# A feature-attention plus Fourier-mixing kernel: the first batch's k, q and v by the hardware queue and TensorE, the trigonometric tables in one chain each, and a new order

## The chip, the cores and the metric

The kernel runs on one core of a Trainium2 chip. The metric is the device time of one execution in microseconds (us), the median of several runs. PE is TensorE, PEld its weight loads, DVE VectorE, ACT ScalarE, POOL GpSimd, SP SyncE.

## What is computed

For 8 batches, 8 heads, 576 positions and 64 columns a head, an attention with a feature map is followed by a Fourier mixing and a two-layer network. The reference, cut to what matters:

```python
def phi(x):
    proj = np.einsum('bhsd,df->bhsf', x, w_phi)          # 64 -> 128
    proj = proj - np.max(np.abs(proj), axis=-1, keepdims=True)
    return np.concatenate([np.exp(proj), np.exp(-proj)], axis=-1)
q_p, k_p = (phi(q), phi(k))
kv = np.einsum('bhsf,bhsd->bhfd', k_p, v)
z = np.sum(k_p, axis=2)
num = np.einsum('bhsf,bhfd->bhsd', q_p, kv)
den = np.einsum('bhsf,bhf->bhs', q_p, z)[..., None] + 1e-06
x = (num / den)                                          # as (8, 576, 512)
X = np.fft.fft(np.fft.fft(x, axis=1), axis=2)
u = x + np.real(X)
un = (u - mean(u)) / np.sqrt(var(u) + 1e-06)
out = u + np.maximum(un @ w_ch1, 0.0) @ w_ch2            # 512 -> 2048 -> 512
```

## The kernel before

All work is done batch by batch, and two to three batches are under way at once. Each batch is cut into streams of small steps, one letter each (`STREAMS`, line 800): K, V and Q load a batch's k, v and q; B and A turn k and q; T makes the feature products (`keys4`, `keys`, `queries`), R the maxima over keys (`kmax`), S the scaled v (`scale_v4`, `scale_v`), P the maxima over queries (`maxima`); M is the mixing (`heads`, then the two transforms), D the folding of rows, N the normalisation, F the two-layer network (`forward`); C makes the constants and W loads the network's weights. The letters of `START`, `FIRST` and seven times `PERIOD` (lines 21 to 23) are the order in which the steps are written, and each engine works through its own instructions in that order. `NEEDS` says which steps must stand ahead of one, and `TILES` and `BUFS` stand for the PSUM buffers (2 of `pj`, 1 of `pk`, 3 of `pb`): `weave` (line 887) holds a letter back until they allow it.

- Loads. POOL's software queue casts fp32 to bf16 on the way (`load`, line 214). For the first batch (`load_first`, line 256) it writes k, v and q in ten pieces. SP then turns k and q by transposing DMAs (`turn_k`, line 270, into `KT4` and `KT`; `turn_q`, line 281).
- Feature products. `keys` (line 349) multiplies a pair of heads of `KT` with `w_phi` into the PSUM tile `psk`; ACT writes both exponentials (`KPp`, `KPn`, line 361); DVE takes the largest absolute value (`MK`, line 375). ACT then makes the scales from `MK` (line 325), and POOL multiplies v by them into `VCn` and `VCp` (line 330; for the first batch DVE does `VCp`). `keyvalue` (line 536) makes `kv` of one head, and ACT copies it as `kvh` (line 552). Queries go the same way through `psq` (maxima `MQ`, line 419) and `psh` (exponentials `QPHP`, `QPHN`, line 469).
- `combine` (line 555) makes one head's output: products on PE, then `tg`, `cb` and `rd` on DVE (lines 566, 571, 573), then the product into `X` on POOL (line 574). Eight of these are followed by the folds `FEO` (line 507) and `CEO`, `SE` (lines 516, 520), which halve the transforms.
- The transforms are matrix products with the tables `CS`, `SS` (576 positions) and `CD`, `SD` (512 columns): `psD` (line 621), `px`, `pu` (line 643). DVE adds `pu` to `X` (lines 648 to 658).
- `normalise` (line 663): per 128 rows DVE takes the statistics (lines 671, 672) and subtracts the mean into `UN` (line 673), and SP transposes `UN` into `UT`. `forward` (line 706) multiplies `UT` with the first weights into `psf` (line 713), ACT applies the ReLU (line 718), the second product is `pso` (line 725), DVE adds it to `X` (line 731), and SP stores.
- The constants (`constants`, line 123) are made on DVE in five chains of three instructions (lines 169, 173, 177), one for each 128 rows of a table, and ACT takes the absolute value (line 181) and the sines (line 195).

Of the kernel before, what the change touches and what calls it, by code (L numbers as in the profile page):

```python
# [20 lines left out]
START = "TSTRCSTSTCSTTCRMMCTKTCRRMPTMRPSTMTNTMMWVRMMMTTMPCTPWDMBNTTTMRPMMMPQMCTAMMNDTMSNSTTTMMRTTSNQRNMRSTTS"  # L21
FIRST = "PMKPTMTFFMFFPMTPPMFRMTPTMTPTFPFFVTRFMMPPTMFFFMFFFMFFAFFMFFPPFMFFTBMFFFMTFFSNFFFFDFFDFQTFTMTFFFFSFSMTFFFMTMFRFTFNFRTMFTFTFFFFTFRMFTFSFTTTFFSFNTTAFNFFFFNFNM"
PERIOD = "MKFMFMPFFMFPMFFMPVFPMBFMMFMFFMFFFRRMFMFFFMFPFFMFTFMFFTFFFPSFTDFFDFFSNSTTFFMFFFFTNFFFMFTMQMFFTFTRRFMTFFTTFFTFNAFSRFMFSFTTFFTFTFTNFFFFFFFNNM"
# [8 lines left out]
def kernel(  # L32
# [71 lines left out]
    gi = xpool.tile([128, 5, C + 1], I32, tag="X", name="gi")  # L104
    gt = [xpool.tile([128, 5, C + 1], F32, tag="X", name=f"gt{i}") for i in range(2)]
    rc_i = gi[:, 0, 0:C]
    pc_i = const.tile([128, 2], I32, name="pc_i")
    rs_i = const.tile([128, 2, 8, 16], I32, name="rs_i")
    tn_i = const.tile([128, 2, 128], I32, name="tn_i")

    def count():
        nc.gpsimd.iota(pc_i[:, 0:1], pattern=[[1, 1]], base=0, channel_multiplier=1)
        nc.gpsimd.iota(rc_i, pattern=[[1, C]], base=0, channel_multiplier=0)
        for j in range(2):
            nc.gpsimd.iota(
                rs_i[:, j], pattern=[[-32, 8], [2, 16]], base=225 + j, channel_multiplier=0
            )
        for t in range(2):
            nc.gpsimd.iota(
                tn_i[:, t, :], pattern=[[1, 128]], base=0, channel_multiplier=2 * t - 1  # L120
            )

    def constants(b):
        rc = gi[:, 1, 0:C].bitcast(F32)
        rs = gi[:, 2, 0:NK].bitcast(F32)
        pc = const.tile([128, 5], F32, name="pc")
        pn = const.tile([128, 5], F32, name="pn")
        blk = const.tile([128, 3], F32, name="blk")
# [17 lines left out]
        nc.vector.tensor_copy(out=rc, in_=rc_i)
        nc.vector.tensor_scalar_add(out=pc[:, 1:2], in0=pc[:, 0:1], scalar1=1.0)
        nc.vector.tensor_scalar_add(out=pc[:, 2:3], in0=pc[:, 3:4], scalar1=256.0)
        nc.vector.tensor_scalar_add(out=pc[:, 4:5], in0=pc[:, 3:4], scalar1=128.0)
        nc.vector.memset(pc[0:1, 2:3], 0.0)  # L150
        nc.vector.tensor_scalar_mul(out=pn[:, 0:3], in0=pc[:, 0:3], scalar1=1.0 / S)
        nc.vector.tensor_scalar_mul(out=pn[:, 3:5], in0=pc[:, 3:5], scalar1=1.0 / C)
        nc.vector.tensor_copy(out=rs[:, 0:256], in_=rs_i[:].rearrange("p j a r -> p (j a r)"))
        nc.vector.tensor_copy(out=rs[:, 256:NK], in_=rc[:, 256:NK])
        nc.vector.memset(rs[:, 256:257], 0.0)
        sins = []
        for j in (3, 4, 0, 1, 2):
            if j < 3:
                n, w, row, P = S, NK, rs, (128, 128, 64)[j]
                dsin, dcos, sgn = SS[0:P, j, :], CS[0:P, j, :], 1.0  # L160
                place = gt[1], 0, 2 * NK * j
            else:
                n, w, row, P = C, C, rc, 128
                dsin, dcos, sgn = SD[:, j - 3, :], CD[:, j - 3, :], -1.0
                place = gt[0], 0, 2 * C * (j - 3)
            t0, t1 = (gi[0:P, i, 0:w].bitcast(F32) for i in (3, 4))
            at = place[0][0:P].rearrange("p a b -> p (a b)")[:, place[2]:place[2] + 2 * w]
            t2, t3 = at[:, 0:w], at[:, w:2 * w]
            nc.vector.tensor_scalar(
                out=t0, in0=row[0:P, 0:w], scalar1=pn[0:P, j:j + 1], scalar2=MAGIC,  # L170
                op0=ALU.mult, op1=ALU.add,
            )
            nc.vector.tensor_scalar(
                out=t1, in0=t0, scalar1=MAGIC, scalar2=-float(n),
                op0=ALU.subtract, op1=ALU.mult,
            )
            nc.vector.scalar_tensor_tensor(
                out=t2, in0=row[0:P, 0:w], scalar=pc[0:P, j:j + 1], in1=t1,
                op0=ALU.mult, op1=ALU.add,
            )  # L180
            nc.scalar.activation(out=t3, in_=t2, func=AT.Abs)
            sc = 2.0 * np.pi / n * (1.0 - 1e-7)
            sins.append((dsin, t2, sgn * sc, 0.0))
            sins.append((dcos, t3, -sc, halfpi[0:P, :]))
            yield
# [69 lines left out]

    def load_first():
        staged["k", 0], pk_ = make_k(0)
        values[0], pv_ = make_v(0, 2)
        staged[0], pq_ = make_q(0)
        load(pk_, (0, 1, 2))  # L260
        nc.gpsimd.memset(V4P[:], 0.0)
        nc.gpsimd.memset(V4N[:], 0.0)
        load(pv_, (2, 0, 1))
        load(pq_, (0,))
        load(pv_, (3,))
        load(pq_, (1, 2, 3))
# [28 lines left out]
    def features(b):  # L295
# [26 lines left out]
        def scale_v(pr):  # L322
            hs = slice(2 * pr, 2 * pr + 2)
            for sgn, VC in ((1.0, VCn), (-1.0, VCp)):
# [4 lines left out]
                eng = nc.vector if b == 0 and sgn < 0 else nc.gpsimd  # L329
                eng.tensor_tensor(  # L330
# [165 lines left out]
    def heads(b):  # L496
# [18 lines left out]
        def fold_rows(cs):  # L515
# [4 lines left out]
            nc.vector.tensor_tensor(  # L520
# [60 lines left out]
        ready = {7: (0,), 6: (1,), 5: (2,), 3: (3,)} if b else {5: (3,), 6: (2,), 7: (1, 0)}  # L581
# [14 lines left out]
    def mixing(b):  # L596
# [6 lines left out]
        nc.scalar.copy(out=CEO[64:128, 2, :, :], in_=pm[64:128])  # L603
# [12 lines left out]
        ET = fpool.tile([128, 2, NK], BF16, tag="ET", name="ET")  # L616
        for i, mat, dst in ((1, SS, ET), (0, CS, DT)):
# [315 lines left out]
```

## Time and profile before

| | us |
|---|---|
| median of 3 runs | 487.97 |
| lowest and highest of them | 486.59 and 494.0 |
| the profiled execution's own time | 493.06 |
| span of its profile, first to last instruction | 491.2 |
| PE busy in the span | 410.0 (83%) |
| DVE, ACT, POOL busy | 330.3, 301.3, 267.2 |

The profiled execution is one run of its own, longer than the median. The span is what the profiler saw from the first to the last instruction; the rest of the time lies around it. Busy time counts what an engine executes; a busy PE is not PE at its peak. Times in the rows further on are counted from the span's start.

### The profile page before, as it was taken

To read this page: it belongs to the slowest core of one execution; us is meant where nothing else is said; L and a number is where in the kernel's file an instruction comes from. 1 tells how busy PE (TensorE), PEld (TensorE's weight loads), DVE (VectorE), ACT (ScalarE), POOL (GpSimd) and SP (SyncE) were. 2 spreads that over 40 slices of the span, in tenths; PEclk is the share of its full clock that TensorE was granted. 3 is DMA by queue.
4 is the path that set the end of the run, shared out by engine and by line. 5 is a ranking of instruction groups with operands and counts; after the bars stand their busy time and mean duration, and the time that the engine had idled before them with its cause. 6 is when DMAs were issued, how large, how long until landed. Compare 5 with 4: busy or idle time off the path is not lost.

```text
span 491.2 us, 10032 instructions
## 1 busy us (share of the span) xinstructions
PE 410.0 (83%) x3897; PEld 250.1 (51%) x3920; DVE 330.3 (67%) x620; ACT 301.3 (61%) x650; POOL 267.2 (54%) x345
## 2 busy tenths in 40 slices
PE   0257271879999899899998999989998999999995
PEld 0135131657447653575456644764375546844752
DVE  1897759457598778586787759775976676739112
ACT  1559453765885689359764786568844977640820
POOL 9434745834945795559547673679356832730100
PEclk9999996798999999899999999999998999999999
DMA  9979993990549917990879265985499024004304
GB/s 105 140 98 173 203 113 54 98 140 2 48 91 125 126 18 103 131 132 9 93 112 144 39 56 101 152 83 45 82 139 123 2 42 104 1 1 79 67 0 97
DMA packets 116303, 42.68 MB, mean 87 GB/s; under 512 B 92576, under 2 KB 111136, under 8 KB 116256
## 3 DMA queue, kind: packets, MB, share of 16 engines
q0 software_dynamic: 52144, 18.37, 37.1%
q1 hardware_dynamic: 64112, 23.67, 30.8%
q8 instruction: 31, 0.51, 0.5%
q14 instruction: 16, 0.13, 0.1%
HBM read 36.77 MB, written 9.44 MB: 94 GB/s over the span
## 4 chain that ended last, share of the span: by engine, by line
PE 50%; DVE 19%; DMA 16%; ACT 9%; POOL 3%; issue 2%; DVEq 0%; SPq 0%; POOLq 0%; ACTq 0%
PE pso L725 18%; PE psf L713 16%; DMA UT<-UN 8%; DMA QT<-QS 4%; PE psD L621 3%; DVE MK L375 3%; DVE UN L673 3%; ACT HT L718 2%; DMA out_dram<-X 2%; DVE st L671 2%; PE pso L740 2%; PE kv L544 2%; DVE cb L571 2%; POOL X L574 1%; ACT KPp L361 1%
## 5 line engine op out<-in xcount | busy, mean ns | idle before, releaser
L713 PE MATMUL psf<-UT,W1b 128*128 128x288 bf16 x1024 | 153.6, 295 | 8.7 <-DMA UT<-UN 7.4
L718 ACT ACTIVATE HT<-psf 128x288 bf16<-128x288 f32 x256 | 103.3, 413 | 81.8 <-PE psf L713 74.4
L725 PE MATMUL pso<-W2b,HT 128*128 128x512 bf16 x491 | 119.4, 380 | 2.9 <-issue 1.1
L713 PEld LDWEIGHTS <-W1b 128*128 128x128 bf16 x1024 | 94.4, 101 | 35.6 <-DMA UT<-UN 6.2
L574 POOL TENSOR_TENSOR X<-cb,rd 128x320 f32<-128x320 f32 x64 | 45.9, 722 | 62.1 <-DVE rd L573 61.6
L725 PEld LDWEIGHTS <-HT 128*128 128x128 bf16 x512 | 46.2, 98 | 59.7 <-issue 10.7
L330 POOL TENSOR_TENSOR VCn<-VS,VCn 128x512 bf16<-128x512 bf16 x32 | 34.5, 1079 | 51.3 <-ACT VCn L325 49.2
L731 DVE SCALAR_TENSOR_TENSOR X<-pso,rs,X 128x512 f32<-128x512 f32 x32 | 23.9, 746 | 45.7 <-PE pso L725 45.7
L507 POOL TENSOR_TENSOR FEO<-X 128x320 f32<-128x320 f32 x60 | 51.9, 885 | 2.4
L419 DVE TENSOR_REDUCE MQ<-psq 128x8 f32<-128x1024 f32 (+1 forms) x40 | 38.8, 1007 | 19.5 <-PE psq L411 19.4
L375 DVE TENSOR_REDUCE MK<-psk 128x8 f32<-128x1024 f32 x32 | 38.4, 1216 | 5.4 <-ACT KPp L361 5.3
L687 POOL TENSOR_SCALAR VE<-MV 128x5 f32<-128x5 f32 x8 | 3.9, 490 | 59.7 <-DVE MV L672 59.6
L361 ACT ACTIVATE KPp<-psk 128x1024 bf16<-128x1024 f32 x32 | 32.5, 1016 | 6.3 <-PE psk L355 5.7
L469 ACT ACTIVATE QPHP<-psh 128x1024 bf16<-128x1024 f32 x32 | 33.2, 1037 | 4.9 <-PE psh L460 4.9
L361 ACT ACTIVATE KPn<-psk 128x1024 bf16<-128x1024 f32 x32 | 32.4, 1012 | 2.3 <-DVE MK L375 2.3
L469 ACT ACTIVATE QPHN<-psh 128x1024 bf16<-128x1024 f32 x32 | 33.5, 1047 | 0.0
L355 PE MATMUL psk<-wphi,KT 64*128 64x128 bf16 x256 | 14.0, 237 | 19.6 <-DVE MK L375 14.9
L330 POOL TENSOR_TENSOR VCp<-VS,VCp 128x512 bf16<-128x512 bf16 x28 | 30.3, 1084 | 0.0
L559 PEld LDWEIGHTS <-QPHP 128*128 128x128 bf16 x320 | 26.3, 105 | 5.8 <-DVE cb L571 3.8
L552 ACT CAST kvh<-kv 128x130 bf16<-128x130 f32 x64 | 17.1, 272 | 18.6 <-PE kv L548 18.4
L671 DVE BATCH_NORM_STATS2 st<-X 128x6 f32<-128x512 f32 (+1 forms) x40 | 27.4, 684 | 0.3
L216 POOL DMA_DIRECT2D QS<-in_q_dram x32 | 26.4, 836 | 0.3 <-issue 0.3
(387 smaller groups left out, 748.3 us busy)
## 6 DMA issues: line engine op xcount, KB each, us to landing
KS<-in_k_dram POOLq DMA_DIRECT2D x16, 256.0 KB, 7.4
QS<-in_q_dram POOLq DMA_DIRECT2D x16, 256.0 KB, 5.0
out_dram<-X SPq DMA_DIRECT2D x64, 64.0 KB
out_dram<-X SPq DMA_DIRECT2D x16, 256.0 KB
VS<-in_v_dram POOLq DMA_DIRECT2D x7, 512.0 KB, 12.2
W1b<-in_moe_w_ch_dram POOLq DMA_DIRECT2D x1, 2048.0 KB, 12.8
W2b<-in_moe_w_ch_dram POOLq DMA_DIRECT2D x1, 2048.0 KB, 24.1
out_dram<-X SPq DMA_DIRECT2D x8, 126.0 KB
```

The source lines that it names most:

```text
L216: nc.gpsimd.dma_start(out=pieces[i][0], in_=pieces[i][1])
L330: eng.tensor_tensor(out=VC[:, hs, :, 0:D], in0=values[b][0][:, hs, :].rearrange("p h (j d) -> p h j d", d=D), in1=VC[:, hs, :, D:D + 1].to ...
L361: nc.scalar.activation(out=KP[:, hs, :, :].rearrange("p e (jp jj) f -> p jj (e jp) f", jj=2), in_=psk[:], func=AT.Exp, scale=sgn,)
L375: nc.vector.tensor_reduce(out=MK[:, 2 * pr:2 * pr + 2, :].rearrange("p e (jp jj) -> p jj (e jp)", jj=2), in_=tiles[pr][:], axis=AX.X, op=A ...
L419: nc.vector.tensor_reduce(out=o, in_=i[:], axis=AX.X, op=ALU.max, apply_absolute_value=True)
L469: nc.scalar.activation(out=o, in_=psh[:], func=AT.Exp, scale=sgn)
L507: eng.tensor_tensor(out=FEO[:, :, i, a:a + D], in0=X[:, :, a:a + D], in1=X[:, :, C - a:C - a - D:-1], op=op,)
L574: nc.gpsimd.tensor_tensor(out=X[:, :, D * h:D * h + D], in0=cb[:, :, 0:D], in1=rd[:].to_broadcast([128, 5, D]), op=ALU.mult,)
L671: nc.vector.bn_stats(out=st[0:M, :], in_=X[0:M, c, 0:C])
L713: nc.tensor.matmul(ps[:], lhsT=W1b[:, cc, 128 * hh:128 * hh + 128], rhs=UT[:, cc, 288 * hf:288 * hf + 288], start=(cc == 0), stop=(cc == N ...
L718: nc.scalar.activation(out=HT[:, hh, 288 * hf:288 * hf + 288], in_=ps[:], func=AT.Relu)
L725: nc.tensor.matmul(po[:], lhsT=HT[:, hh, 128 * c:128 * c + 128], rhs=W2b[:, hh, :], start=(hh == 0), stop=(hh == NHH - 1),)
```

## The change

The first batch's k, q and v come by SP's hardware queue as fp32, without a cast, into memory that is not yet in use (the second weights' tile `W2b` and the network's tile `HT`). TensorE turns k and q there: ten parts of four 128-column blocks (`turn_part`), each part copied out of PSUM as bf16 by ACT (the first two) or DVE. The steps of these parts are two new streams, G (k) and J (q). v is read as fp32 by the products on POOL, which now makes both `VCn` and `VCp`.

Each kind of table has one chain: the 576-position tables as one tile 960 wide, the 512-column tables for the first 128 rows alone; the second 128 rows are made on POOL from the first by a quarter turn (`CD` and `SD` exchanged, with signs). The last table rows are used to partition 65 instead of 128.

In the first batch, the mean is subtracted by ACT instead of DVE, one fold goes from POOL to DVE, half of `SE` goes from DVE to POOL, and the query weights are made in two halves. P has an empty seventh step for the other batches. The three strings of the order are new.

```diff
-START = "TSTRCSTSTCSTTCRMMCTKTCRRMPTMRPSTMTNTMMWVRMMMTTMPCTPWDMBNTTTMRPMMMPQMCTAMMNDTMSNSTTTMMRTTSNQRNMRSTTS"
+START = "CGGTCRTGGRJJGSSTTTWCSTTTPRMTTTRMTKPJRRSTPRJDMTMJSPQPTMMMTMPMWTMSMTMTMMMTBTMMPVMTRCCMTNNRADTNMTNNSSMSSNMTQTMR"
...
+        t0 = gc[:, C:2 * C]
...
+        nc.vector.tensor_tensor(
+            out=at.rearrange("p (j n) -> p j n", n=NK),
+            in0=rs.unsqueeze(1).to_broadcast([128, 3, NK]),
+            in1=pc[:, 0:3].unsqueeze(2).to_broadcast([128, 3, NK]), op=ALU.mult,
+        )
...
+            nc.gpsimd.tensor_tensor(
+                out=dst[:, 1, a::2].rearrange("p (n t) -> p n t", t=2),
+                in0=src[:, 0, a::2].rearrange("p (n t) -> p n t", t=2),
+                in1=sign, op=ALU.mult,
+            )
...
     def load_first():
-        load(pk_, (0, 1, 2))
...
-        load(pv_, (2, 0, 1))
-        load(pq_, (0,))
-        load(pv_, (3,))
-        load(pq_, (1, 2, 3))
...
+        def put(out, in_):
+            nc.sync.dma_start(out=out, in_=in_)
+
+        put(KF4, k[0, :, 512:576, :].rearrange("h p d -> p h d"))
+        for e in range(2):
+            put(wphi_f[64 * e:64 * e + 64, :], w_phi[:, :])
+        for g in range(2):
+            hs = slice(4 * g, 4 * g + 4)
+            put(KF[:, hs, :], k[0, hs, 0:512, :].rearrange("h (p j) d -> p h (j d)", j=4))
+        for QF, at in ((Q01, 1), (Q23, 320)):
+            put(QF, q[0, :, at:at + 256, :].rearrange("h (p j) d -> p h (j d)", j=2))
...
+    def turn_part(dst, blocks, by_act):
+        P = blocks[0].shape[0]
+        ps = pb.tile([128, 4, P], F32, tag="pb", name="pst")
+        for x, block in enumerate(blocks):
+            nc.tensor.transpose(ps[:, x, :], block, ident[0:P, 0:P])
+        if by_act:
+            nc.scalar.copy(out=dst, in_=ps[:])
+        else:
+            nc.vector.tensor_copy(out=dst, in_=ps[:])
...
-                eng = nc.vector if b == 0 and sgn < 0 else nc.gpsimd
-                eng.tensor_tensor(
+                nc.gpsimd.tensor_tensor(
                     out=VC[:, hs, :, 0:D],
...
-        ready = {7: (0,), 6: (1,), 5: (2,), 3: (3,)} if b else {5: (3,), 6: (2,), 7: (1, 0)}
+        ready = {7: (0,), 6: (1,), 5: (2,), 3: (3,)} if b else {6: (3,), 7: (2, 1, 0)}
...
+            if b == 0:
+                nm = small.tile([128, 1], F32, tag="nm", name="nm")
+                nc.vector.tensor_scalar_mul(out=nm[0:M, :], in0=mv[0:M, c, 0:1], scalar1=-1.0)
+                nc.scalar.activation(
+                    out=UN[0:M, c, :], in_=X[0:M, c, 0:C], func=AT.Identity, bias=nm[0:M, :]
+                )
```

Three places on DVE show the new order. The first is DVE's queue around the first batch's key maxima (`MK` of the pairs of heads). Before, chains of the tables stand between them (`gi`, `gt`):

```order
L169 TENSOR_SCALAR gi<-gi,pn 128x320
L173 TENSOR_SCALAR gi<-gi 128x320
L177 SCALAR_TENSOR_TENSOR gt_119<-gi,pc 128x320
L375 TENSOR_REDUCE MK<-psk 128x2x4
L330 TENSOR_TENSOR VCp<-VS,VCp 128x8x64
L169 TENSOR_SCALAR gi<-gi,pn 128x320
L173 TENSOR_SCALAR gi<-gi 128x320
L177 SCALAR_TENSOR_TENSOR gt_119<-gi,pc 128x320
L169 TENSOR_SCALAR gi<-gi,pn 64x320
```

In the changed kernel the last table instruction and the copies of the transposed parts (`pst`) stand there:

```order
L180 TENSOR_TENSOR gs<-gs 128x960
L456 TENSOR_REDUCE MK_151<-ps_196 128x4
L331 CAST KT<-pst 128x512 x2
L461 TENSOR_REDUCE MK<-psk 128x2x4
L331 CAST QT_143<-pst 128x512
L331 CAST QT_144<-pst 128x512
L331 CAST KT<-pst 128x512
```

All table chains now lie ahead of the first key maximum, `VCp` has left DVE, and five copies of parts came in.

The second is DVE's queue where the first batch's mixed rows (`pu`) arrive and are normalised. Before:

```order
L375 TENSOR_REDUCE MK<-psk 128x2x4
L648 TENSOR_TENSOR X<-pu,X 128x512
L651 TENSOR_TENSOR X<-pu,X 128x511
L654 TENSOR_TENSOR X<-pu,X 128x1
L671 BN_STATS st<-X 128x6
L672 BN_AGGR MV_113<-st 128x2
L673 TENSOR_SCALAR UN<-X,MV_113 128x512
L671 BN_STATS st<-X 128x6
```

Now:

```order
L461 TENSOR_REDUCE MK<-psk 128x2x4
L742 TENSOR_TENSOR X<-pu,X 128x512
L745 TENSOR_TENSOR X<-pu,X 128x511
L748 TENSOR_TENSOR X<-pu,X 128x1
L765 BN_STATS st<-X 128x6
L766 BN_AGGR MV_110<-st 128x2
L769 TENSOR_SCALAR nm<-MV_110 128x1
L765 BN_STATS st<-X 128x6
```

The 512-wide subtraction into `UN` became a one-column negation `nm`, and the subtraction itself stands on ACT.

The third is DVE's queue in a later period, where one batch's second product (`pso`) meets the next batch's statistics. Before:

```order
L673 TENSOR_SCALAR UN<-X,MV_113 128x512
L731 SCALAR_TENSOR_TENSOR X<-pso,rs,X 128x512
L671 BN_STATS st<-X 128x6
L672 BN_AGGR MV_113<-st 128x2
L673 TENSOR_SCALAR UN<-X,MV_113 128x512
L731 SCALAR_TENSOR_TENSOR X<-pso,rs,X 128x512
L747 SCALAR_TENSOR_TENSOR X<-pso,rs,X 64x512 x2
```

Now:

```order
L774 TENSOR_SCALAR UN<-X,MV_110 128x512
L832 SCALAR_TENSOR_TENSOR X<-pso,rs,X 128x512 x2
L765 BN_STATS st<-X 128x6
L766 BN_AGGR MV_110<-st 128x2
L774 TENSOR_SCALAR UN<-X,MV_110 128x512
L848 SCALAR_TENSOR_TENSOR X<-pso,rs,X 64x512 x2
```

The statistics of the fourth 128 rows now stand behind both additions of `pso` instead of between them.

## Rows read from the trace of the kernel before

**Rows 1.** Windows of the whole span: busy us per engine, granted clock, DMA share, GB/s.
```profile
0.00:52.00 52.00, 20.01 (x245) 14.65 (x245) 34.53 (x80) 31.29 (x60) 29.70 (x47) 1.00 1.01 133
52.00:104.00 52.00, 27.47 (x270) 16.58 (x272) 31.37 (x63) 27.22 (x57) 30.06 (x37) 0.87 0.92 114
...
104.00:456.00 352.00, 332.87 (x3194) 200.80 (x3213) 259.32 (x472) 230.57 (x505) 205.72 (x260) 0.98 0.65 80
```

**Rows 2.** Waits between 0 and 100 us, the longest: total, times, longest.
```profile
PE psk L355 <- DVE MK L375: 14.9, 3, 7.1
```

**Rows 3.** Windows of the first batch by stage, columns as in rows 1.
```profile
16.00:44.96 28.96, 14.51 (x172) 10.36 (x169) 23.37 (x35) 21.90 (x46) 13.94 (x16) 1.00 0.85 125
44.96:59.43 14.47, 5.50 (x78) 4.30 (x76) 11.14 (x29) 8.45 (x14) 9.62 (x13) 1.00 1.26 203
59.43:71.25 11.82, 7.29 (x36) 3.00 (x37) 6.59 (x17) 5.11 (x13) 5.50 (x8) 1.00 1.16 152
71.25:87.26 16.01, 5.58 (x63) 3.28 (x62) 15.62 (x29) 7.72 (x15) 9.79 (x12) 0.70 0.42 56
```

**Rows 4.** Timeline from 0 to 45 us: start, us, engine, line, operation, idle time before it.
```profile
0.73 1.23 SPq L80 DMA_DIRECT2D wphi_f<-in_w_phi_dram  x2
...
3.58 0.45 DVE L81 CAST wphi<-wphi_f 128x128 bf16<-128x128 f32 x1 [2.42 <-DMA wphi_f<-in_w_phi_dram]
...
10.66 0.60 ACT L346 ACTIVATE K4p<-ps 128x512 bf16<-128x512 f32 x1 [8.65 <-PE ps L341]
...
16.00 1.02 ACT L361 ACTIVATE KPp<-psk 128x1024 bf16<-128x1024 f32 x1 [4.26 <-PE psk L355]
...
22.38 1.60 POOL L330 TENSOR_TENSOR VCn<-VS,VCn 128x512 bf16<-128x512 bf16 x1 [2.03 <-issue]
...
22.98 1.18 DVE L169 TENSOR_SCALAR gi<-gi,pn 128x320 f32<-128x320 f32 x1
...
42.77 1.03 PE L426 MATMUL pt<-MQ,TURN 128*128 128x16 f32 x4
...
44.96 0.50 DVE L566 TENSOR_TENSOR tg<-pn__521,E 128x325 f32<-128x325 f32 x1 [0.85 <-ACT E L433]
```

**Rows 5.** Windows of two microseconds, for the DMA columns at their right end.
```profile
4.00:6.00 2.00, 0.00 (x0) 0.00 (x0) 0.03 (x1) 0.00 (x0) 2.00 (x4) 1.00 0.98 87
...
44.00:46.00 2.00, 1.07 (x17) 0.79 (x14) 1.11 (x3) 1.98 (x4) 0.00 (x0) 1.00 1.06 217
```

**Rows 6.** Groups by line and form from 0 to 80 us: busy us, mean ns.
```profile
L375 DVE TENSOR_REDUCE MK<-psk 128x8 f32<-128x1024 f32 x6 | 7.3, 1213 | 3.8 <-ACT KPp L361 3.8
L361 ACT ACTIVATE KPp<-psk 128x1024 bf16<-128x1024 f32 x7 | 7.2, 1023 | 4.6 <-PE psk L355 4.6
...
L419 DVE TENSOR_REDUCE MQ<-psq 128x4 f32<-128x512 f32 x8 | 5.1, 681 | 2.2 <-PE psq L411 2.2
...
L330 DVE TENSOR_TENSOR VCp<-VS,VCp 128x512 bf16<-128x512 bf16 x4 | 4.6, 1158 | 2.2 <-ACT VCp L325 2.2
...
L673 DVE TENSOR_SCALAR UN<-X,MV 128x512 bf16<-128x512 f32 x4 | 2.0, 509 | 0.1
...
L181 ACT ACTIVATE gt<-gt 128x512 f32<-128x512 f32 x2 | 1.3, 628 | 0.0
```

**Rows 7.** Timeline from 50 to 88 us: what stands at the bounds of rows 3.
```profile
50.87 0.46 DVE L566 TENSOR_TENSOR tg<-pn__612,E 128x325 f32<-128x325 f32 x1
...
59.43 1.04 DVE L516 TENSOR_TENSOR CEO<-FEO 128x256 bf16<-128x256 f32 x1
...
71.25 0.69 DVE L648 TENSOR_TENSOR X<-pu,X 128x512 f32<-128x512 f32 x1 [0.56 <-PE pu L643]
...
87.26 2.11 PE L713 MATMUL psf<-UT,W1b 128*128 128x288 bf16 x8
```

**Rows 8.** Waits of PE from 152 to 414 us, the longest: total, times, longest.
```profile
PE psf L713 <- DMA UT<-UN: 7.4, 4, 2.3
```

**Rows 9.** Timeline of the last batch's end: an addition of `pso` and the idle time before it.
```profile
480.46 0.75 DVE L731 SCALAR_TENSOR_TENSOR X<-pso,rs,X 128x512 f32<-128x512 f32 x1 [2.70 <-PE pso L725]
```

More of the change, by code (lines that the diff above doesn't have):

```diff
@@ L103 @@
     V4N = const.tile([128, 4, 2, D + 1], BF16, name="V4N")
[L104 to L113 removed]
+    gc, gs, ga = (
+        xpool.tile([128, 5, C + 1], F32, tag="X", name=n)[:].rearrange("p a b -> p (a b)")
+        for n in ("gc", "gs", "ga")
+    )
@@ L114, in count, with count_all @@
+    def count_all():
+        for t in range(2):
+            count(tn[:, t, :], [[1, 128]], 0, 2 * t - 1)
+        nc.vector.tensor_single_scalar(
+            out=ident[:], in_=tn[:, 0, :], scalar=0.0, op=ALU.is_equal
+        )
+        count(pc_i[:, 0:1], [[1, 1]], 0, 1)
+        count(pc[:, 3:4], [[1, 1]], 0, 1)
+        count(rc, [[1, C]], 0, 0)
+        count(pc[:, 0:2], [[1, 2]], 225, 2)
         for j in range(2):
-            nc.gpsimd.iota(
-                rs_i[:, j], pattern=[[-32, 8], [2, 16]], base=225 + j, channel_multiplier=0
-            )
@@ L118, in count @@
[L118 to L121, printed above, removed]
-    def constants(b):
[L124 to L128, printed above, removed]
+            count(
+                rs[:, 128 * j:128 * j + 128].rearrange("p (a r) -> p a r", r=16),
+                [[-32, 8], [2, 16]], 225 + j, 0,
+            )
@@ L154, in constants @@
[L154 to L185, printed above, removed]
@@ new lines, in turn_part, with turn_first_k @@
+    def turn_part(dst, blocks, by_act):
[7 more added lines that the diff above has]
+            nc.vector.tensor_copy(out=dst, in_=ps[:])
+    def turn_first_k(b):
+        KF, KF4 = raw[0][0:2]
+        KT, KT4 = turned_k[0]
+        turn_part(KT4[:], [KF4[:, 2 * x:2 * x + 2, :].rearrange("p h d -> p (h d)") for x in range(4)], True)
+        yield
+        for pr in range(4):
+            turn_part(
+                KT[:, 4 * pr:4 * pr + 4, :],
+                [KF[:, 2 * pr + x // 2, 128 * (x % 2):128 * (x % 2) + 128] for x in range(4)],
+                pr < 1,
+            )
+            yield
@@ L270, in turn_k, with turn_first_q @@
+    def turn_first_q(b):
+        Q01, Q23, QF4 = raw[0][2:5]
+        QT01, QT23, QT4 = turned_q[0]
+        for g in range(2):
+            for QF, QT in ((Q01, QT01), (Q23, QT23)):
+                turn_part(QT[:, 4 * g:4 * g + 4, :], [QF[:, 4 * g + x, :] for x in range(4)], False)
+                yield
+            if g == 0:
+                turn_part(QT4[:], [QF4[:, 2 * x:2 * x + 2, :].rearrange("p h d -> p (h d)") for x in range(4)], False)
+                yield
     def turn_k(KS, KS4):
@@ L519, in fold_rows @@
             )
-            nc.vector.tensor_tensor(
+            eng = nc.gpsimd if b == 0 and cs.start == 0 else nc.vector
+            eng.tensor_tensor(
                 out=SE[:, :, cs], in0=FEO[:, 0:2, 0, cs], in1=FEO[:, 2:4, 0, cs], op=ALU.add
@@ L602, in mixing @@
         )
-        nc.scalar.copy(out=CEO[64:128, 2, :, :], in_=pm[64:128])
+        nc.scalar.copy(out=CEO[64:65, 2, :, :], in_=pm[64:65])
         nc.vector.scalar_tensor_tensor(
@@ L820 @@
         "P": lambda b, i, n: (
-            n("A", b) >= 1 and n("M", b - 2) >= 16 and (i < 5 or n("C", 0) >= 6)
+            n("A", b) >= 1 and n("M", b - 2) >= 16 and (i not in (3, 6) or n("C", 0) >= 3)
+            and (b or n("J", 0) >= (1, 2, 3, 3, 4, 5, 5)[i])
         ),
```

212 lines of the change are left out of this document (145 added, 67 removed).

## The prediction

> **What bounds the kernel now.** I read the windows of the whole span first. From 104 to 456 us PE is busy 332.87 of 352.00 us, so that stretch has little to give; from 0 to 104 it is busy 47.5 of 104 [rows 1]. The changed code lies almost all in that head. Next I read the waits of the head: the longest is PE at a key product `psk`, 14.9 us in three waits for DVE's key maxima `MK` [rows 2]. So DVE's queue sets the pace there, and the stage windows say how closely: from the first key exponential (16.00) to the first combination `tg` (44.96) DVE is busy 23.37 of 28.96 us and ACT 21.90; from the arrival of the mixed rows (71.25) to the first product of the network (87.26) DVE is busy 15.62 of 16.01 [rows 3, 4, 7]. The timeline tells what comes before: ACT sits idle 8.65 us until `K4p` at 10.66, and the first key product's exponential starts at 16.00 [rows 4].
>
> **The sum's frame.** The profiled execution took 493.06 us (span 491.2), the median of the runs is 487.97, 5.1 less. The sum is made against 493.06 and 5.1 is taken off at the end, as the execution-to-execution part.
>
> **Term A, up to the first `tg` (before: 44.96).** SP spends 1.23 us on two loads, 0.62 each, and `w_phi`, issued at 0.73, is used at 3.58, 2.85 us later [rows 4]. The small piece of k is now first, so it is there at about 3.6. The first half of k is the fourth load, issued at 0.73 + 3 x 0.62 = 2.6; with what is ahead of it 0.7 MB have to move. No fp32 copy from memory stands in the trace. The software queue wrote 217 GB/s at its best and 87 while starting [rows 5]: 3.3 or 8.3 us, so landing at 6 or 11. I take 6, since the 87 belong to a queue that was only filling. All 3.6 MB take 17 us at 217, and the last v is there at about 20; the second half of v is wanted later than that.
>
> A part is four transpositions of fp32 blocks. The nearest row is `pt`, two fp32 products in four passes of 0.26 us (1.03 in all) [rows 4]. From below, 288 columns with their weights take 0.26 us (2.11 for eight), 128 at that rate 0.12 [rows 7]; from above two passes, 0.52. A part costs 0.5 to 2.1 us; I take 1.2, a little over one pass a block. So k's first full part is ready at 7.2, its copy on ACT (0.63, as a 512-wide pass over SBUF [rows 6]) at 7.8, then `K4p`, `K4n` 0.60 each and the 960-wide absolute value (0.63 x 960 / 512 = 1.2): the first `KPp` starts at 10.2 instead of 16.00.
>
> From there to `tg` it took 28.96 us, 5.6 more than DVE's 23.37. What is each engine's work now? DVE loses `VCp` (4.6) and eleven table instructions that lay in this stretch (at 0.6 each, half of the one in rows 4, 7), and gains eight copies of parts (at most 0.63 each, 5.0): about 17. ACT loses up to five absolute values (3.1) and two 1.02 us exponentials that now stand behind `tg`: about 17. POOL takes over the four `VCp` at 1.16: 13.94 + 4.6 = 18.6, with the next batch's q loads for its v loads [rows 3, 6]. The busiest is now POOL with 18.6. I keep the 5.6 us of waits, because a new one replaces the old: twenty transpositions (five parts, letters GGRJJG, 6 us) stand on PE between the first and the second key product, while ACT has about 4 us of other work. So `tg` comes at 10.2 + 18.6 + 5.6 = 34.4. A = 10.6. Bounds: parts at 2.1 put 0.9 + 4.5 us back (5.2); parts at 0.5 and half of the waits gone give 14.
>
> The Trainium skill ("TensorE: Matmul & The Clock Gate", Part 4: PE-mode transpose) gives about 275 ns for a 128x128 transposition in a kernel (390 alone), of bf16; that would be 1.1 a part, and A would be 11.2. No row here shows one.
>
> One row speaks against the move of work beside POOL: a 320-wide pass on DVE took 1.18 us beside a `VCn` on POOL that itself took 1.60 [rows 4], where the 512-wide subtraction into `UN` on DVE takes 0.51 [rows 6]. The Trainium skill ("SBUF — State Buffer", Who interferes with whom) has DVE and GpSimd share one pair of ports, so that one fully blocks the other. The row agrees. By that rule the 960-wide chain, which now runs beside POOL's counting and clearing, would be some 1.5 us longer, and A 9.1.
>
> **Term B, from `tg` to the mixed rows (26.29 us).** A combination takes (50.87 - 44.96) / 5 = 1.18 us [rows 4, 7], eight of them 9.5, and they still do. The other 5.0 us of the first window [rows 3] are the folds, each of which waited for `X` on POOL between the last combinations. Now all but one stand behind the eighth; `X` (0.7) and five half-microsecond folds on DVE make 3.4. That is 1.6 gained. In the second window the clearing of table rows and half of `SE` leave DVE (some 1.9), but two `MK` of 1.21 come in: 0.5 lost. The quarter turns on POOL are hidden behind these; if they were not, they would be late by their four products of about half a `VCp`, 2.3 us. B = 1.1, bounds -1.5 and 3.
>
> **Term C, from there to the network (16.01 us).** DVE is the bound. Five subtractions of 0.51 go to ACT, five one-column negations (0.1) come: 2.0. Two of the three `MK` of this window now lie ahead: 2.4 [rows 6]. C = 4.4. ACT takes 5 x 0.63 = 3.1 us more in a window where it is busy 7.72 of 16.01 [rows 3]: covered. Without cover it is back to 1.3; and if the network starts as soon as its first three transposed row blocks are there, ahead of the last statistics, 6.5.
>
> **Given back.** Of the ten query maxima of the second batch some four (0.6 each) ran ahead of the network's start on DVE; now all stand behind: 2.4. What follows is bound by PE at 95% [rows 1], so the rest of the gain reaches the end. The new order of the periods I cost at nothing: the wait for `UT`, 7.4 us in four waits [rows 8], can go or be doubled.
>
> **Sum.** 10.6 + 1.1 + 4.4 - 2.4 = 13.7; 493.06 - 13.7 = 479.4, less 5.1 is 474. A change under 2%, 9.8 us, is about what a measurement of this kernel cannot tell from none; 478.2 is that line.
>
> **Rivals.**
> 1. The first loads or the transpositions become the wait. For it: no fp32 load is in the trace, its runs are 256 to 1024 bytes, and five parts stand between two key products. At 87 GB/s q would land at 30 and the last v at 44, `tg` would follow at about 47, and A = -2: total 493.06 - (-2 + 1.1 + 4.4 - 2.4) - 5.1 = 487. Parts at 2.1 us give A = 5.2 and 480. Against: 217 GB/s were written while the source gave twice that in fp32. Between the two, 484.
> 2. Slower: the period's order. In each later batch DVE now takes the statistics of the fourth 128 rows behind both additions of `pso` instead of between them. If those rows' `UT` is what the second half of the network waits for, each batch waits one block of `pso` longer, 2.70 + 0.75 = 3.45 us [rows 9]. For seven batches that is 24 us: 474 + 24 = 498. It outweighs the gain of the head from 2 us a batch. Against: the last 64 rows of `UT` come later still and have kept their place, and the wait for `UT` was under 2 us a batch.
> 3. More than forecast: A 14, B 1.1 and C 6.5, with the waits for `UT` halved (3.7): 493.06 - 5.1 - 22.9 = 465.
>
> **Chances.** Forecast 0.60 (468 to 479), rival 1 0.22 (479 to 488), rival 2 0.05, rival 3 0.13. Faster by over 2% takes the forecast but for its edge, rival 3 and the best end of rival 1: 0.70; within 2% the rest of rival 1: 0.25; slower 0.05. The range 465 to 485 leaves out rival 2, the worst of rival 1 and a little below.
>
> **What would show it.** In the profile after: `K4p` starts near 8 and the first `KPp` near 10; twenty transpositions take 4 to 8 us; `tg` starts at 32 to 37; the first `psf` 14 to 18 us earlier than 87.26; PE's share from there to the end as before; and the distance from the first `psf` to the end at most 3 us longer than 404. It is wrong if `tg` is later than 40 (rival 1: then PE or a load is named before `psk`), or if the head is shorter and the distance from `psf` to the end longer by as much (rival 2: PE's wait for `UT` above 20 us).

## The result, and the profile after

| | before | after |
|---|---|---|
| median (lowest to highest), us | 488.42 (486.59 to 494.0) | 461.56 (458.98 to 463.53) |
| ratio, 95% interval | | 0.9459 [0.9382, 0.9536] |
| profiled execution, its span | 493.06, 491.2 | 458.98, 457.1 |

The change gains 26.9 us between the medians; the forecast was 14, its range ended at 465. Between the two profiled executions the difference is 34.1. (The ratios compare fast executions alone; left out are, among others, one of e1 with 1372 us, one of e18 with 492.5 and two of the five of e12 with 600 at a granted clock of 0.65 throughout, of which e12's profile is one and is not read.)

The windows of the changed kernel that answer to [rows 1]:

```profile
0.00:52.00 52.00, 29.79 (x325) 21.72 (x325) 40.44 (x82) 36.77 (x67) 36.92 (x65) 0.71 1.09 177
52.00:104.00 52.00, 40.09 (x439) 25.82 (x442) 34.91 (x69) 35.40 (x80) 34.64 (x49) 0.83 0.80 100
104.00:456.00 352.00, 339.48 (x3178) 202.31 (x3197) 246.91 (x448) 230.99 (x505) 195.81 (x245) 1.00 0.60 82
```

PE does 22.4 us more of its work ahead of 104. But it is also busier behind 104, at a granted clock of 1.00 instead of 0.98, where I had said that PE's share stays. The stages of the changed kernel, bounded by the same events as in [rows 3] (first `KPp`, first `tg`, first `CEO`, first `X`, first `psf`, end):

```profile
10.49:33.48 22.99, 17.33 (x196) 12.77 (x194) 16.66 (x26) 18.31 (x40) 17.17 (x20) 0.70 0.91 182
33.48:47.51 14.03, 7.04 (x98) 5.61 (x99) 12.16 (x31) 11.44 (x16) 10.78 (x15) 0.59 1.61 145
47.51:60.12 12.61, 7.30 (x28) 2.49 (x29) 6.51 (x11) 5.64 (x12) 8.84 (x19) 0.51 1.30 190
60.12:69.04 8.92, 3.10 (x34) 1.48 (x33) 7.96 (x22) 5.80 (x13) 7.25 (x8) 0.87 0.28 54
69.04:457.10 388.06, 370.46 (x3558) 224.29 (x3580) 271.84 (x490) 257.17 (x567) 218.67 (x276) 0.99 0.61 83
```

The column of the granted clock cannot be compared between the two kernels here: before, it reads 1.00 up to 71 us, yet eight 128-column products take 0.61 us there (`psk` at 21.05), as long as in the changed kernel under 0.50 (`psq` at 20.82).

The last stretch in the kernel before:

```profile
87.26:491.20 403.94, 375.79 (x3542) 228.13 (x3561) 268.74 (x486) 255.77 (x562) 216.37 (x273) 0.98 0.63 78
```

Stage by stage, beside the terms of the sum:

| | before | after | gain | forecast |
|---|---|---|---|---|
| A, start to first `tg` | 44.96 | 33.48 | 11.5 | 10.6 |
| B, to the first `X` | 26.29 | 26.64 | -0.35 | 1.1 |
| C, to the first `psf` | 16.01 | 8.92 | 7.1 | 4.4 |
| from there to the end | 403.94 | 388.06 | 15.9 | -2.4 |
| sum | | | 34.1 | 13.7 |

So the head was read nearly right, and the miss lies behind the first `psf`, where 10.5 us of the 15.9 are PE's idle time (28.15 to 17.60) and 5.3 its busy time. The longest waits of PE between 104 and 456 us, in the kernel before:

```profile
PE psf L713 <- DMA UT<-UN: 7.4, 4, 2.3
PE psq L411 <- DMA QT<-QS: 3.5, 4, 1.8
PE ph L439 <- DVE MK L375: 2.3, 4, 0.6
```

and in the changed kernel:

```profile
PE ps L427 <- DMA KT<-KS: 1.4, 1, 1.4
PE psq L497 <- DMA QT<-QS: 1.4, 2, 0.7
PE psf L814 <- DMA UT<-UN: 1.1, 2, 0.9
```

The busy time shrinks with the dips of the clock, which are gone. In the kernel before, the windows with two of those waits show them (granted clock third from the right; 0.50 is the lower of its two levels), and the timeline shows what follows a wait:

```profile
200.00:208.00 8.00, 6.24 (x78) 4.27 (x77) 3.88 (x7) 2.97 (x10) 6.16 (x8) 0.79 1.12 136
204.00:206.00 2.00, 2.00 (x18) 1.45 (x17) 0.84 (x1) 0.93 (x3) 2.00 (x4) 0.50 0.98 121
264.00:272.00 8.00, 6.02 (x59) 4.45 (x58) 3.58 (x11) 2.99 (x8) 6.19 (x9) 0.79 1.72 141
```

```profile
203.18 0.40 PE L411 MATMUL psq<-wphi,QT 64*128 64x128 bf16 x8 [1.76 <-DMA QT<-QS]
203.50 1.80 PE L713 MATMUL psf<-UT,W1b 128*128 128x288 bf16 x8
```

Eight products into `psf` take 1.14 us elsewhere, here 1.80 after a wait of 1.76. There are four such dips behind 104 us, three behind waits for `QT` or `UT` of 1.76 to 2.26 us and one behind two shorter waits for `MQ`. In the changed kernel every window of 8 us between 104 and 448 reads 1.00.

### The profile page after: what moved, and what is told of

Read it like the earlier page. It is cut to its first block, busy times and chain, and to the rows that moved or that the text cites. A ratio compares the mean times of both kernels' runs of the same rounds, so it can differ in the third digit from the quotient of the medians.

```text
span 457.1 us, 10115 instructions
## 1 busy us (share of the span) xinstructions
PE 409.4 (90%) x3941; PEld 249.9 (55%) x3964; DVE 322.3 (71%) x597; ACT 303.2 (66%) x651; POOL 267.4 (58%) x357
## 4 chain that ended last, share of the span: by engine, by line
PE 65%; DMA 11%; DVE 9%; ACT 6%; POOL 5%; issue 2%; SPq 0%; DVEq 0%; ACTq 0%; POOLq 0%
PE pso L826 24%; PE psf L814 16%; PE pu L737 4%; DMA UT<-UN 3%; DMA QT<-QS 3%; PE psD L715 3%; PE kv L637 3%; PE pso L841 2%; PE psh L547 2%; POOL FEO L599 2%; DMA KT<-KS 2%; ACT HT L819 2%; PE psk L441 2%; PE psq L497 2%; ACT KPp L447 1%
## 5 line engine op out<-in xcount | busy, mean ns | idle before, releaser
L814 PE MATMUL psf<-UT,W1b 128*128 128x288 bf16 x1024 | 148.9, 288 | 6.9 <-DMA UT<-UN 4.6
L814 PEld LDWEIGHTS <-W1b 128*128 128x128 bf16 x1024 | 92.5, 98 | 32.3 <-issue 10.0
L599 POOL TENSOR_TENSOR FEO<-X 128x320 f32<-128x320 f32 x59 | 49.6, 862 | 2.2
L416 POOL TENSOR_TENSOR VCn<-VS,VCn 128x512 bf16<-128x512 bf16 x28 | 29.8, 1066 | 34.3 <-ACT VCn L412 32.6
L652 PEld LDWEIGHTS <-QPHP 128*128 128x128 bf16 x320 | 24.8, 102 | 5.5 <-DVE cb L664 4.3
L652 PEld LDWEIGHTS <-QPHN 128*128 128x128 bf16 x320 | 23.2, 99 | 1.3 <-issue 0.2
L237 POOL DMA_DIRECT2D QS<-in_q_dram x28 | 23.1, 837 | 0.3 <-issue 0.3
```

Of the source, the lines that this page charges most:

```text
L416: nc.gpsimd.tensor_tensor(out=VC[:, hs, :, 0:D], in0=values[b][0][:, hs, :].rearrange("p h (j d) -> p h j d", d=D), in1=VC[:, hs, :, D:D + ...
L599: eng.tensor_tensor(out=FEO[:, :, i, a:a + D], in0=X[:, :, a:a + D], in1=X[:, :, C - a:C - a - D:-1], op=op,)
L652: nc.tensor.matmul(pn_[:, i, 65 * c:65 * c + 65], lhsT=QP[:, h, 128 * c:128 * c + 128], rhs=kvh[:, i, :], start=True, stop=True,)
L814: nc.tensor.matmul(ps[:], lhsT=W1b[:, cc, 128 * hh:128 * hh + 128], rhs=UT[:, cc, 288 * hf:288 * hf + 288], start=(cc == 0), stop=(cc == N ...
```

## The experiments: which string

**e1** puts back the string of the later periods (with an empty step for P), **e2** that of the first batch's network, **e3** puts the new periods' string into the kernel before, and **e4** puts the query maxima back.

```diff
e1 -PERIOD = "MKFMFFMFPMFP...NNNFM"    +PERIOD = "MKFMFMPFFMFP...FNFFFFFFFNNM"
e2 -FIRST = "PMFTKMPT...NNFMS"         +FIRST = "PMKPTMTF...NFNM"
e3 (before) -PERIOD = "MKFMFMPF...NNM" +PERIOD = "MKFMFFMF...NNNFM"
e4 -(0,0) (1,0) qmax4 ... (0,1) (1,1)  +(0,0) (0,1) (1,0) ... (1,1) qmax4   (b > 0)
```

> The changed kernel with only the string of the later periods put back (an empty step added to it). Theory 1, the new order of the periods makes the stretch behind the first psf 16 us shorter: seven periods get back 2 to 3 us each, 474 to 479 us against 461.6 for the changed kernel, and PE's waits for UT and QT are back at 8 us or more, with dips of the granted clock. Theory 2, the shorter stretch follows from the head (a network that starts earlier finds its rows ready): 461 to 465, no new waits.

> The changed kernel with only the string of the first batch's network (FIRST) put back, two empty steps added. Theory 1 says that the seven later periods carry the gain: 461 to 466, with what is lost before 110 us. A rival, that the first period's order sets how far each batch runs ahead and so all later ones: 470 or more.

> The kernel before with only the string of the later periods taken from the changed kernel (the empty step left out; maxima in their old order). Theory 1: 488 less 14 to 16, 472 to 474, with the head as it was (first psf at 87) and PE's waits for UT at most 3 us. Theory 2: 486 to 490. If the new order needs the new order of the maxima to work, something between, near 480.

> The changed kernel with the five query maxima of the batches behind the first in their old order (first half of the rows for all heads, then the second, the 64 rows last); strings unchanged. Theory 1 in its plain form, the order of the letters does it: 461 to 464. If the order of the maxima carries the gain of the periods: 468 to 478, with PE waiting for QT at psq.

Ratios to the kernel before: e1 0.9558 [0.9466, 0.9649], e2 0.9571 [0.9513, 0.9629], e3 0.9824 [0.9729, 0.9919], e4 0.9364 [0.9273, 0.9454]. Of 490 us the new periods are worth 8.6 in the old kernel (e3) and 5 in the new one by the ratios (0.9558 against 0.9459, with intervals that overlap; 8 by the profiles, 465.1 against 457.1). PE's waits for `UT` and `QT` in e1 are 6.1 and 4.4 us, about as before. So theory 1 is right in kind, but both runs missed its numbers: e1 lies below 474 and e3 above 474, near the 480 that was put down to a need for the new order of the maxima, and e4 speaks against such a need. One reason is that e1's execution has no dip of the clock, while the four dips before cost some 6.7 us (the missing clock of its 8 us windows). The waits bring the dips in some executions only.

FIRST is worth 5.5 (8.5 by the profiles), against theory 1. Its first place is in the head; in e2 the first `psf` stands behind a maximum and comes at 71.61 instead of 69.04, though its first `X` is ready 1.25 us earlier (58.87); the rest of the 5.5 lies behind and was not followed:

```profile
70.13 0.58 PE L497 MATMUL psq<-wphi,QT 64*128 64x128 bf16 x7 [3.59 <-DVE MQ L505]
71.61 2.11 PE L814 MATMUL psf<-UT,W1b 128*128 128x288 bf16 x8
```

The order of the maxima (e4) shows no gain.

## Which place in the period

The two strings have cuts at which the same letters lie behind them. **e5** puts back the first 34 letters, **e7** the next 67, **e6** the last 38; of these **e13** all but the last eleven, **e12** the last eleven.

```diff
e12 -FFFFFFNNNFM
e12 +NFFFFFFFNNM
```

> The changed kernel with only the first 34 letters of the later periods' string put back (there the first query maximum stands behind two network products instead of four). If the place of the maxima keeps PE from waiting for QT: the wait for QT goes from 1.4 back to 4 us or more, 463 to 466 us. If the end of the string carries the gain: 458 to 462.

> The changed kernel with only the last 38 letters of that string put back (there one of the last statistics stands further ahead, and the queries' steps stand among the products of the second half). If the end carries the gain: PE's wait for UT goes from 1.1 back to 5 us or more, 464 to 468. If not: 458 to 462. This would also answer my rival 2, which took the new place of the fourth 128 rows' statistics for a loss: then the old place is faster, 450 to 457.

> The changed kernel with only the middle 67 letters put back. Theory 1 in its narrow form has nothing at stake there but PE's short waits of ph for MK (2.3 us in four): 460 to 464. If 466 or more, the gain of the order is spread over the whole period.

> The changed kernel with only the last eleven letters of the later periods put back: DVE again takes the statistics of the fourth 128 rows between the two additions of pso, and SP transposes those rows ahead of the 256 KB store instead of behind it. This is the move that my rival 2 took for a loss. Theory 3, it is the gain: the store is out of the way before the last two transpositions into UT, which land earlier, and without it PE waits for UT 5 us or more and the time is 468 to 474. If rival 2 had been right in sign: 440 to 457. If neither: 459 to 463, and the gain lies in the 27 letters ahead (next run).

> The changed kernel with the 27 letters ahead of those put back (places of the queries' steps, of the scaled v and of the third statistics among the products of the second half). Theory 3: 459 to 464. If the place of the queries' steps is what counts: 467 to 474, with PE waiting for UT or for MK.

e5 0.9431 [0.9353, 0.9508], e7 0.9395 [0.9326, 0.9463] and e13 0.9435 [0.9338, 0.9532] stay at the changed kernel's ratio; e6 0.9650 [0.9553, 0.9747] and e12 0.9617 [0.9482, 0.9752] lose it. e13 and e12 ran on the same chip: 0.0182 x 490 = 9 us; e12's ratio rests on two executions and the intervals just overlap, while those of e6 and e13 do not. The gain of the periods hangs on one letter: the statistics of the fourth 128 rows, behind both additions of `pso` instead of between them. That is the move of my rival 2, with the opposite sign. The profile of e6 has PE waiting for `UT` 7.1 us in three waits again.

## Why that place

On SP the move lets the 256 KB store of one batch's fourth rows go ahead of the transposition of the next batch's fourth rows. **e15** undoes this on SP alone, **e14** puts DVE's order back and only SP's transposition behind the stores, **e16** is e12 with the next load of v later, **e17** the changed kernel again.

```diff
e15  -            store(b, U, c)
e15  +            if c < 3 or b in (0, 7): store(b, U, c)    # c = 3 just ahead of store(b, U, 4)
e14  (e12) the dma_start_transpose of c = 3 moved to the start of norm(4)
e16  (e12) -...FPVMFPB...MFFMFFFMM  +...FPMFPB...MVFFMFFFMM
```

> The changed kernel, DVE's order untouched, but the 256 KB store of the fourth 128 rows issued behind the transposition of the next batch's fourth rows, just ahead of the 126 KB store, as SP's queue had it before. If the place of the store is the cause: 466 to 474 and PE's wait for UT 5 us or more. If DVE's order is the cause: 457 to 463.

> The kernel of e12 (statistics of the fourth 128 rows between the additions) with one thing put back as the changed kernel has it: SP issues the transposition of those rows behind the 256 KB store, together with that of the last 64 rows. If the place of the store in SP's queue is the cause: back to 457 to 463, PE's wait for UT 3 us or less. If DVE's order itself is the cause: 467 to 474, like e12.

> The kernel of e12 with the next batch's v loaded later (behind the second product into X instead of right behind its k), so that 0.58 MB less are under way when the last 64 rows are transposed. If the late landing of the last UT is a matter of what else moves at that time: 458 to 464, PE's wait for UT half or less of e6's 7.1. If it is a matter of SP's queue alone: 467 to 474. V itself should not be missed: its scaled products come 20 us later.

> The changed kernel unaltered, to be compared with the other runs of this call on the same chip: 459 to 463, and the scatter of its executions.

e17 gives 0.9463 [0.9393, 0.9532], e15 0.9649 [0.9581, 0.9716]: the store's place alone costs 9 us, with DVE's order untouched. PE's waits for `UT` behind 104 us, e15 and then e17:

```profile
PE psf L814 <- DMA UT<-UN: 10.3, 4, 3.9
```

```profile
PE psf L814 <- DMA UT<-UN: 3.2, 3, 2.2
```

So the cause is the place of the store in SP's queue. One period of e15, SP's queue (256 KB, 126 KB and 2 KB stores at L802, L804 and L805) and the product that waits:

```profile
231.42 1.23 SPq L778 DMA_TRANSPOSE UT<-UN  x1
232.70 0.65 SPq L802 DMA_DIRECT2D out_dram<-X  x1
233.44 0.42 SPq L804 DMA_DIRECT2D out_dram<-X  x1
233.92 0.29 SPq L805 DMA_DIRECT2D out_dram<-X  x1
234.30 2.87 SPq L778 DMA_TRANSPOSE UT<-UN  x1
```

```profile
246.01 2.08 PE L814 MATMUL psf<-UT,W1b 128*128 128x288 bf16 x8 [3.93 <-DMA UT<-UN]
```

and the same place in the changed kernel:

```profile
231.09 0.65 SPq L802 DMA_DIRECT2D out_dram<-X  x1
231.83 1.31 SPq L778 DMA_TRANSPOSE UT<-UN  x1
233.24 0.45 SPq L804 DMA_DIRECT2D out_dram<-X  x1
233.75 0.26 SPq L805 DMA_DIRECT2D out_dram<-X  x1
234.10 1.19 SPq L778 DMA_TRANSPOSE UT<-UN  x1
```

```profile
242.51 1.14 PE L814 MATMUL psf<-UT,W1b 128*128 128x288 bf16 x8 [0.87 <-DMA UT<-UN]
```

The last transposition is issued at nearly the same time, but its issue takes 2.87 us instead of 1.19, and the product starts 11.7 us after it instead of 8.4. In this period PE runs slower behind the wait (2.08 for eight, granted clock 0.50 from 246 to 248 us). The Trainium skill ("DMA: Bandwidth & Descriptors", Queues, rings and completion order) says that the descriptors of one issuing queue are taken in the order of issue on each DMA engine, which takes turns between queues; by it, what stands ahead in SP's queue is ahead of the transposition, while POOL's loads (issued at 232.57 in e15, 232.13 in the changed kernel) take their share. The trace agrees in sign; no run shows the packets themselves. Whether the store acts by its place in the queue's order or by moving its bytes 1.6 us later, beside the last transposition, stays open.

e14 missed: 0.9661 [0.9556, 0.9767], no return, since there both last transpositions stand behind all three stores (3.53 to 3.68 us to issue both). e16, 0.9592 [0.952, 0.9663], lies between and decides nothing: `UT` still costs 4.4 us, intervals overlap, and e19 below shows the later v to have a price of its own.

## The head, by its terms

**e10** puts `VCp` of the first batch on DVE, **e8** the first half of `SE`, **e9** the subtraction of the mean.

```diff
e10 +  eng = nc.vector if b == 0 and sgn < 0 else nc.gpsimd
e8  -  eng = nc.gpsimd if b == 0 and cs.start == 0 else nc.vector
e9  -  if b == 0:    (nm on DVE, Identity on ACT)
e9  +  if b < 0:
```

> The changed kernel with the four VCp of the first batch on DVE again (1.16 each in the trace of before). My term A took DVE's loss of 4.6 us as part of what makes the first 34 us shorter, with POOL as the new bound. If DVE is still the pace: tg 3 to 4.6 us later, 464 to 466. If POOL is: tg earlier or unchanged, 457 to 462.

> The changed kernel with the first half of SE of the first batch on DVE again, for 0.5 us there. In the trace of the changed kernel it ran on POOL behind the next batch's loads and the quarter turns, and DVE waited 2.35 us for it. If that wait is on the path to the network: first psf 1.5 to 2.3 us earlier, 457 to 460. If something else comes as late (the sum pm waits for HI on ACT): no change, 460 to 463.

> The changed kernel with the mean of the first batch subtracted on DVE again, five passes of 0.51 us for five one-column passes of 0.15. This stretch came out 2.7 us shorter than my term C. If the subtraction on ACT is worth what I said (2.0) the first psf comes 1.5 to 2 us later, 462 to 464; if ACT's copy was as late as DVE (three transpositions are what the first psf waits for), no change, 460 to 462.

e10, 0.9546 [0.9462, 0.9631], with its first `tg` 5.3 us later than 33.48 and a span 5.6 longer:

```profile
38.78 0.49 DVE L660 TENSOR_TENSOR tg<-pn__547,E 128x325 f32<-128x325 f32 x1
```

So DVE's queue still sets this stage, not POOL as I had it: from the first `KPp` to `tg` POOL is busy 13.7 us instead of 17.2, and nothing comes earlier for it. In this execution the whole delay reaches the end; the intervals of the ratios overlap.

e8, 0.9405 [0.9345, 0.9465], its first `psf` 0.2 us earlier: the time lies where a gain was expected, but the `psf` and the overlapping intervals do not show one. In the changed kernel the wait for `SE` looks like the bound, with `HI` on ACT ahead of it:

```profile
48.91 0.58 PE L692 MATMUL pm<-HI,ones_b 1*128 1x512 bf16 x1 [4.57 <-ACT HI L621]
53.64 0.71 POOL L613 TENSOR_TENSOR SE<-FEO 128x256 f32<-128x256 f32 x1
54.39 0.69 DVE L697 SCALAR_TENSOR_TENSOR CEO<-pm,SE 128x512 bf16<-128x512 f32 x1 [2.35 <-POOL SE L613]
```

In e8 the same instruction of DVE came 0.6 us earlier and waited for ACT's half of `CEO` instead; the next thing was as late.

e9, 0.9495 [0.9421, 0.9569], 1.6 to 4 us in the time (459.1 to 461.6 against 463.2, within the scatter), but 6.9 us at the first `psf` (75.97 against 69.04). Part of the reason stands in DVE's and POOL's rows, e9:

```profile
62.83 1.21 DVE L774 TENSOR_SCALAR UN<-X,MV 128x512 bf16<-128x512 f32 x1
...
64.90 1.35 DVE L774 TENSOR_SCALAR UN<-X,MV 128x512 bf16<-128x512 f32 x1
...
68.37 0.93 DVE L774 TENSOR_SCALAR UN<-X,MV 128x512 bf16<-128x512 f32 x1
...
70.14 0.49 DVE L774 TENSOR_SCALAR UN<-X,MV 128x512 bf16<-128x512 f32 x1
```

```profile
62.71 1.06 POOL L416 TENSOR_TENSOR VCp<-VS,VCp 128x512 bf16<-128x512 bf16 x1
63.72 1.24 POOL L416 TENSOR_TENSOR VCn<-VS,VCn 128x512 bf16<-128x512 bf16 x1
```

Beside POOL's scaled v the subtraction takes 1.21 and 1.35 us, and 0.49 once POOL is through (my 0.51 was the free case). ACT's copy takes 0.72 beside the same work of POOL. The third subtraction is the last that the first `psf` needs; it ends at 69.30 instead of 66.58. That is 2.7 of the 6.9 us. The rest lies behind it, between its transposition and the product, in e9:

```profile
69.33 1.19 SPq L778 DMA_TRANSPOSE UT<-UN  x1
75.97 1.12 PE L814 MATMUL psf<-UT,W1b 128*128 128x288 bf16 x4 [7.16 <-DMA UT<-UN]
```

and in the changed kernel:

```profile
65.86 0.72 ACT L770 ACTIVATE UN<-X,nm 128x512 bf16<-128x512 f32 x1 [1.39 <-DVE nm L769]
66.61 1.19 SPq L778 DMA_TRANSPOSE UT<-UN  x1
69.04 1.12 PE L814 MATMUL psf<-UT,W1b 128*128 128x288 bf16 x4 [3.45 <-DMA UT<-UN]
```

The product starts 6.6 us after the issue instead of 2.4. POOL issues the next batch's q loads from 68.1 us (68.3 in the changed kernel), so in e9 the transposition comes behind them and in the changed kernel ahead; that these loads delay it is a guess that no run tests.

## A version that may be faster

**e18** is the changed kernel with the 126 KB and 2 KB stores behind the last transposition too, and `SE` as in e8; **e19** adds the later load of v.

```diff
-        store(b, U, 4)
+        if b in (0, 7): store(b, U, 4)
+        else: late.append((b, U))       # stored in normalise(b + 1), behind norm(4)
```

> The changed kernel with the 126 KB and 2 KB stores of a later batch issued behind the next batch's last transposition into UT (and the first half of SE on DVE, which e8 showed at nothing to 2 us). If a store right ahead of a transposition delays it, the last one now comes 0.7 us earlier at its issue and lands sooner: PE's wait for UT under 1 us behind 104 us, 454 to 458 against 459 to 462 for the changed kernel. If only the 256 KB store counts: 458 to 461, as e8.

> The kernel of e18 with the next batch's v loaded later, as in e16. If what moves beside the last transposition still costs something: below e18 by 1 to 2 us, 453 to 457. If nothing is left to gain there: as e18.

e18 has the best ratio of both kernels and all but e4 of the variants, 0.9381 [0.9312, 0.945] (median 456.52), where the changed kernel's two were 0.9459 and 0.9463: about 4 us less, as expected, though the intervals overlap, and `SE` alone (e8) came within about 1 us of it. The wait it aimed at, 1.1 and 3.2 us in the two traces of the changed kernel, is nearly gone:

```profile
PE psf L819 <- DMA UT<-UN: 0.3, 1, 0.3
```

That the small stores count too fits this wait; the time does not show it. e19 is 0.9484 [0.9439, 0.953], 5 us worse, with intervals that barely overlap; its place for v costs more than it frees, and why was not tried.

## Why the prediction was wrong, point by point

- **Term A held** (11.5 against 10.6). Its steps in the changed kernel:

```profile
6.90 1.11 PE L327 MATMUL pst<-ident,W2b 128*128 128x128 f32 x4 [2.55 <-DMA W2b<-in_k_dram]
...
9.23 2.82 PE L327 MATMUL pst<-ident,W2b 128*128 128x128 f32 x12
12.28 1.07 PE L327 MATMUL pst<-ident,W2b 128*128 128x128 f32 x8 [0.23 <-DMA W2b<-in_q_dram]
...
18.49 0.40 PE L441 MATMUL psk<-wphi,KT 64*128 64x128 bf16 x8 [3.50 <-DVE MK L461]
```

```profile
8.62 0.60 ACT L432 ACTIVATE K4p<-ps 128x512 bf16<-128x512 f32 x1
...
10.49 1.03 ACT L447 ACTIVATE KPp<-psk 128x1024 bf16<-128x1024 f32 x1
```

  The first half of k is there at 6.90 (said: 6), `K4p` at 8.62 (7.8), `KPp` at 10.49 (10.2), twenty transpositions take 4.1 us (6). The first part took 1.11, as 1.2 was said, eight later transpositions 1.07. So rival 1 fell. One step in it was wrong though the sum was not: DVE's queue sets the stretch (e10), not POOL, and the busiest engine is ACT (18.31 us, POOL 17.17, DVE 16.66). So it is partly luck that POOL's 18.6 and 5.6 of waits, 24.2 in all, came near the 22.99 measured. The wait for `MK` [rows 2] is down to 3.5. That no fp32 load is in the trace overlooked the two of `w_phi` [rows 4]; nothing in the sum hung on it. What of A the loads and transpositions bring and what the tables bring, no run separates.
- **Term B failed by 1.4 us.** "The quarter turns on POOL are hidden": they are not, `SE` stood behind them and DVE waited 2.35 us, the bound that the step had named (2.3). e8 shows that removing this wait alone brings nothing, since ACT's half is as late.
- **Term C was undersized** (7.1 against 4.4). Two things: the case that I kept as a bound, that the network starts as soon as its three row blocks are there, is what FIRST does (with the old one, e2, the stretch from the first `X` takes 12.7 us instead of 8.9, and in the changed kernel none of the three `MK` is left in it, where I had left one); and the first three subtractions on DVE would have cost 0.93 to 1.35 instead of 0.51 beside POOL's load, which the new order puts at the same time (e9).
- **"The new order of the periods I cost at nothing" is the step that failed**. It was worth 8 to 9 us of the time (e3, e13 against e12, e15 against e17); the stretch behind the first `psf` came out 15.9 us shorter between the two profiles, where I had it 2.4 longer. I had the wait for `UT` in hand [rows 8] and asked only which engine is late; the transposition into `UT` came late by what stood ahead of it in SP's queue, not by an engine (e15: 9 us for one store's place). The dips of the clock behind the waits, some 6.7 us in the profile before, were not in the sum at all. And rival 2 priced the very move that brings the gain as a loss of 3.45 us a batch, because it followed DVE's order and never SP's.
- **"Given back" did not show**: the query maxima behind the network's start cost nothing that the stretch shows, perhaps because FIRST hides them; FIRST itself gains 5.5 (e2), of which the sum counted nothing.
- **The frame.** The profiled execution before was 5.1 above its median, that after 2.6 below. Against medians the head and its strings make the larger part of 26.9 us: 8 to 9 come from the periods' order (e3, e12), 5.5 from FIRST, and the 13 left are near the forecast's 13.7, if these parts add up, which no run shows.

## What to carry to other kernels

When a change moves letters of a hand-written order, read each queue's own sequence, the DMA-issuing queue first: the place of one store among the transpositions was worth 9 us here, without any engine's instruction moved. A short wait on PE can have a second price, the slow pace behind it: four waits of 2 us can cost more than 8 us, though e1 and e6 had such waits without a dip. Before costing a pass on DVE, see what POOL does at the time at which the pass will run.

## What the runs showed of the hardware

- Passes of DVE over 128x512 fp32 in SBUF (the subtraction) went from 0.49 to 1.35 us beside POOL's products (e9), while the statistics between them kept 0.68. The Trainium skill ("SBUF — State Buffer", Who interferes with whom) says that single-input passes of this kind can take a mode that locks the ports that DVE and GpSimd share, and that ACT never waits; the rows agree on both.
- Issuing the last transposition of a batch, which stands behind the two small stores, took 1.18 to 1.61 us in all seven later batches of the changed kernel. In e15, with the 256 KB store just ahead of these two, it took 2.17 to 2.87 us in four of the six batches concerned, and PE waited for `UT` in these four. A long issue is not needed for a wait: e17 has one of 2.2 us behind an issue of 1.21.
- fp32 transpositions of 128x128 took 0.235 us each (2.82 for twelve) and then 0.134 (1.07 for eight), and eight 128-column products 0.61 us (`psk` at 8.69) and then 0.40 (13.28), without a change in the granted clock's column, which reads 1.00 in all these stretches. In the kernel before, such products take 0.61 us as late as 69 us under 1.00. Ahead of its first fall (between 76 and 78 us before, between 18 and 20 in the changed kernel) the column was no guide to the pace.
